# Sigmoid attention and two gated MLPs in one kernel: scores and value sums on one ring of four double PSUM banks, with fewer and longer bursts of sums

## The chip, the cores and the metric

The kernel runs on one core of a Trainium2 chip. The metric is the device time of one execution in microseconds (us), the median of several runs. The core's engines are named as in the profile: PE (TensorE, the matrix multiplies), DVE (VectorE), ACT (ScalarE), POOL (GpSimd) and SP (SyncE, which here only issues transfers). Each engine works through its own queue in order; one engine waits for another by counting semaphores. PSUM holds what PE writes; in this kernel it is handed out as "banks" of 512 floats per partition, eight in all, alone (`[P, 512]`) or as a double bank (`[P, 2, 512]`).

## The reference, cut to what matters

```
def attention(q, k, v):                        # q, k, v: (4 batches, 12 heads, 448, 64)
    scores = matmul(q, k.T) / sqrt(64) - log(448)
    return matmul(sigmoid(scores), v)          # no softmax, each weight stands alone

def gated_mlp(x, w_in, w_sp, b_sp, w_out, act):
    h = act(x @ w_in)                          # 768 -> 1024
    u, v = h[..., :512], h[..., 512:]
    v = (v - mean(v)) / sqrt(var(v) + 1e-6)    # the second MLP also: * g_ln
    v = einsum('ts,bsd->btd', w_sp, v) + b_sp[None, :, None]
    return (u * v) @ w_out                     # 512 -> 768

x = attention(q, k, v), heads side by side     # (4, 448, 768)
x = gated_mlp(x, ..., relu)
x = x + gated_mlp(x, ..., gelu_tanh)
```

## The kernel before, in words

**Parts.** Attention runs first. Then come the first MLP (`m1`) over the four batches, then a part in which the first MLP's output matrix and the second one's input matrix are multiplied into one, then the second MLP (`m2`). All products are of single-precision accuracy: most are made as three passes over operands split into a high part of a shorter format and a low part (`hi`, `lo`).

**Groups, pairs and units.** A *group* n is four heads of one batch (batch n // 3), so there are twelve; two groups n (even) and m = n + 1 make a *pair*, and there are six pairs. The 448 keys are cut into three row blocks of 128 and a rest of 64. A *unit* of scores (n, r) holds row block r of the four heads of a group, 24 matmuls (three passes by two halves of the head's 64 numbers by four heads, line 485). The rests of both groups of a pair are one unit of their own, (n, 3), 16 matmuls (line 503). So a pair has seven units, 42 in all. The very first unit, (0, 0), is made without splitting, from line 470.

**What follows a unit.** ACT takes the sigmoid of the unit's four banks with two instructions (`weigh`, line 452), which write the weights `a` (three buffers) or, for the rests, `ar` (one). PE then multiplies them with the values: `values(n, r, x)`, line 519, is a *slot* of two matmuls, for heads 2x and 2x + 1; x is the *half* of the group. Over r = 0, 3, 1, 2 a half's sums gather in one PSUM bank. When they are done, `gather(n, x)` lets ACT copy them (line 533) into a chunk of the next stage's input `x`. Even batches need one copy for a half; odd batches lie rotated in their tile and need four.

**Banks.** In attention two single banks (`ps_av`) hold the sums of the two halves, and three double banks (`ps_att`) hold scores, two for a unit. `ps_av` stays for the MLPs; `ps_att` is closed after the last unit of scores and its space is given to the pools `ps_sc` and `ps_t`.

**Order.** The order of PE's work in attention is written out by hand: a list `units` gives the order of the score units, and a table (`todo`, made into `sums`) says which slots of value sums stand behind each unit. The loop at the end of `attention` issues for each step s first `score(s)`, then `weigh_up(s)`, the *burst* of sums; then come DVE's preparation of later groups (`turn`: transposes; `high`, `low`: the split) and the next loads. PE runs its queue in the order in which it was issued.

**Weights.** The MLPs' weights arrive as 64-bit floats and are converted piece by piece by DVE and ACT. A `Belt` holds the jobs and each `tick` moves each running job on by a step and starts new ones. In attention the belt's jobs are `convert_early` (14 pieces of `w_in1`, at the steps that `rate` names); in the first MLP they are the pieces in `out1` (12 pieces of 256 columns of `w_out1`, stored to a matrix `flat` in DRAM), then those of `w_in2`, moved on by `fill`. `spatial` is such a belt for the matrix `w_sp`.

**The seam to the MLP.** After the last unit `done()` runs (`operands_made`): it closes attention's operand pool and `ps_att`, and issues the casts of the first batch's input (`split_x`: `xh` on ACT, `xl` on DVE). The last group's sums are copied by `gather_last`, which the program calls behind the first wide projection, `m1.hv(0, 0)` (18 matmuls, line 656):

```
            m1.hv(0, 0)
            gather_last()
            fill(1)
            for b in range(B):
                ...
                for j in range(0 if b else 1, J):
                    m1.hv(b, j)
                    fill(2 if j == J - 1 else 1)
```

`m1.hu` (line 702) makes the four blocks of `u` of a batch, `m1.sp` (line 722) the spatial product.

Of the kernel before, what the change touches and what calls it, by code (L numbers as in the profile page):

```python
# [9 lines left out]
F32 = mybir.dt.float32  # L10
# [16 lines left out]
def tile_sigmoid_attention_two_gated_mlps(  # L27
# [49 lines left out]
    ps_av = ctx.enter_context(tc.tile_pool(name="ps_av", bufs=2, space=bass.MemoryType.PSUM))  # L77
# [4 lines left out]
    xs = [const.tile([P, KF, 2 * S], F32, name=f"x{i}") for i in range(B // 2)]  # L82
    xe = [
        const.tile([P, KD - KF, 2 * S], F32, tag=f"xe{i}", name=f"xe{i}", bufs=1) for i in range(B // 2)
    ]

    def chunk_of(b, c):
        return xs[b // 2][:, c] if c < KF else xe[b // 2][:, c - KF]
# [9 lines left out]
    def av_bank():  # L98
        return ps_av.tile([P, 512], F32, tag="av", name="av")
# [54 lines left out]
    def convert_early(apool, src, n, size, part):  # L154
# [25 lines left out]
        f = f.bitcast(F32)  # L180
        hi, lo = part()
# [145 lines left out]
    out1 = pieces_kept(w_out1, 0, rows_of(flat))  # L327
# [4 lines left out]
    def attention(apool, epool, ps_att, done):  # L332
        G = H // 4
        NG = B * G
        raws, turned, ops, vs, att, avp = {}, {}, {}, {}, {}, {}

        def load_qk(n, xs="kq"):
            b, i = divmod(n, G)
# [9 lines left out]
        def load_v(n):  # L348
            b, i = divmod(n, G)
# [100 lines left out]
        def weigh(a, sc):  # L450
            for dst, src in sc:
                nc.scalar.activation(a[:, dst], src[..., :S], AF.Sigmoid, bias=bias_s, scale=scale)  # L452

        def pairs(sc):
            return [(slice(2 * x, 2 * x + 2), sc[x]) for x in range(2)]

        def scores(n, r):


            opk, opq = ops[n]  # L460
            if (n, r) == (0, 0):
                t, *av = ps_att.tile([P, 2, 512], F32, tag="sc", name="sc"), av_bank(), av_bank()
                banks = [t[:, 0], t[:, 1], *av]
                parts = [(2, av[0]), (3, av[1]), (slice(0, 2), t)]
# [11 lines left out]
            else:  # L476
                sc = score_banks()
                banks = [x[:, h] for x in sc for h in range(2)]
                parts = pairs(sc)
# [10 lines left out]
            att[n, r] = a = epool.tile([P, 4, S], F32, tag="a", name="a", bufs=3)  # L490
            weigh(a, parts)

        def scores_rest(n):


            sc = score_banks()
# [12 lines left out]
            weigh(a, pairs(sc))  # L509

        def values(n, r, x):
            if r == 0:
                avp[n, x] = av_bank()
            vt, vr = vs[n]
            at = REST * ((x + n) % 2)
            ps = slice(at, at + REST)
            for o in range(2):
                h = 2 * x + o
                nc.tensor.matmul(  # L519
                    avp[n, x][o * D:(o + 1) * D, :S],  # L520
                    vt[:, h, r] if r < 3 else vr[ps, o], att[n, r][:, h] if r < 3 else att[n, r][ps, h],
                    start=(r == 0), stop=(r == 2),
                )

        def gather(n, x):

            b, i = divmod(n, G)
            y = chunk_of(b, 2 * i + x)
            o = avp.pop((n, x))[:, :S].rearrange("p (c t) -> p t c", c=TC)

            def back(at, t0, t1, c0=0, c1=TC):
                dst = y[:, at:at + (t1 - t0) * (c1 - c0)]
                nc.scalar.copy(
                    out=dst.rearrange("p (t c) -> p t c", t=t1 - t0), in_=o[:, t0:t1, c0:c1]
                )
# [13 lines left out]
        for n in range(0, NG, 2):  # L549
            m, at = n + 1, len(units)  # L550
            units += [(n, 0), (n, 1), (n, 3), (n, 2), (m, 0), (m, 1), (m, 2)]
            both = lambda n, r: [(n, r, 0), (n, r, 1)]
            todo = (
                [(n, 0, 0)], [(n, 0, 1), (n, 1, 0)], [(n, 1, 1)] + both(n, 3), both(n, 2),
                both(m, 0), both(m, 3) + [(m, 1, 0)], [(m, 1, 1), (m, 2, 0)], [(m, 2, 1)],
            )
            if n == 0:
                todo = [both(0, r)[::-1] for r in (0, 1, 3, 2)] + list(todo[4:])
            for s, x in enumerate(todo, at + 1):
                sums.setdefault(s, []).extend(x)  # L560
# [27 lines left out]
        warm = av_bank()  # L588
# [31 lines left out]
        def gather_last():  # L620
            for x in range(2):
                gather(NG - 1, x)

        return gather_last


    class Mlp:
# [82 lines left out]
        def sp(self, b, i):  # L710
# [14 lines left out]
            if L.n == 1:  # L725
# [3 lines left out]
                    out=xs[b // 2][:, i, o:o + S], in0=t, in1=u, op=ALU.mult  # L729
# [397 lines left out]
```

## Time and profile before

| | |
|---|---|
| three runs | 556.13, 556.19, 556.82 us, median 556.19 |
| the profiled execution | 556.78 us, its span 555.0 us |
| busy share of the span | PE 99%, PEld (weight loads) 79%, DVE 65%, ACT 40%, POOL 6% |
| granted TensorE clock, mean | 0.999 |
| attention, 0 to 139.7 us | PE 138.35, DVE 107.16, ACT 96.51 us busy |
| first MLP, 139.7 to 291 us | PE 150.80, DVE 131.05, ACT 60.71 us busy |
| the two matrices made one, 291 to 324 us | PE 33.00, DVE 24.46, ACT 8.84 us busy |
| second MLP, 324 to 551.5 us | PE 227.49, DVE 96.96, ACT 54.90 us busy |

The times are those of one core, so the span is its span; 1.78 us of the profiled execution lie around it. A stage ends where PE's first matmul of the next one starts. Busy PE includes the time in which its pipeline fills and empties.

### The profile page before, as it was taken

How to read it: one execution, taken by the hardware profiler on the slowest of the kernel's cores; microseconds unless marked ns; L12 is line 12 of the kernel's file. 1: busy time of each engine (PE TensorE's matmuls, PEld its weight loads, DVE VectorE, ACT ScalarE, POOL GpSimd, SP SyncE). 2: the span in 40 equal slices, each digit the busy share in tenths (PEclk: the TensorE clock that was granted, in tenths of full speed). 3: DMA queues.
4: the chain of work that ended last, by engine and by line, in shares of the span. 5: the costliest groups of instructions: out<-in, count | busy, mean ns of one | idle time of the engine just before them, and what ended most of it. 6: DMA issues, size and time to landing. Idle time of an engine off the chain costs nothing.

```text
span 555.0 us, 9160 instructions
## 1 busy us (share of the span) xinstructions
PE 549.6 (99%) x3486; PEld 436.6 (79%) x3486; DVE 360.1 (65%) x753; ACT 221.0 (40%) x404; POOL 32.5 (6%) x62
## 2 busy tenths in 40 slices
PE   9999999999999999999999999999999999999997
PEld 5544445444798898898998889998999899989886
DVE  6999888850699999999865977951542264224311
ACT  5667676677434252361543156310320041113101
POOL 0000000000110100300100011000100020011000
PEclk9999999999999999999999999999999999999999
DMA  8788647200443265463445534200500032004003
GB/s 286 213 239 253 190 137 244 77 21 18 72 126 128 96 190 121 119 156 91 150 144 137 145 109 123 75 0 9 79 15 0 9 57 36 1 16 65 6 1 113
DMA packets 96107, 56.44 MB, mean 102 GB/s; under 512 B 67392, under 2 KB 84032, under 8 KB 96064
## 3 DMA queue, kind: packets, MB, share of 16 engines
q1 hardware_dynamic: 95920, 55.60, 37.0%
q8 instruction: 27, 0.44, 0.3%
q10 hardware_dynamic: 144, 0.26, 0.1%
q14 instruction: 16, 0.13, 0.1%
HBM read 44.83 MB, written 11.01 MB: 101 GB/s over the span
## 4 chain that ended last, share of the span: by engine, by line
PE 94%; DVE 2%; DMA 1%; issue 1%; ACT 1%; SPq 1%; POOL 0%; DVEq 0%; POOLq 0%; ACTq 0%
PE t L702 15%; PE t L656 14%; PE av L519 13%; PE sc L788 10%; PE sc L485 9%; PE t L722 6%; PE av L788 5%; PE av L722 3%; PE sc L722 3%; PE sc L798 3%; PE t L884 3%; PE av L884 3%; PE sc L503 2%; PE av L798 2%; PE t L798 2%; DMA w<-in_moe_w_out_dram 1%
## 5 line engine op out<-in xcount | busy, mean ns | idle before, releaser
L452 ACT ACTIVATE a<-sc,small 128x896 f32<-128x896 f32 x71 | 67.7, 1005 | 32.6 <-PE sc L485 32.6
L519 PE MATMUL av<-a,vt 128*64 128x448 f32 x288 | 63.0, 554 | 0.0
L485 PEld LDWEIGHTS sc<-opq,opk 32*128 32x128 f32 x840 | 38.4, 183 | 25.7 <-issue 13.4
L665 DVE BATCH_NORM_STATS2 st<-vr 128x6 f32<-128x512 f32 x28 | 19.4, 692 | 60.2 <-ACT vr L662 60.2
L485 PE MATMUL sc<-opq,opk 32*128 32x448 f32 x840 | 52.7, 378 | 0.0
L662 ACT ACTIVATE vr<-t 128x512 f32<-128x512 f32 x28 | 16.7, 596 | 84.3 <-PE t L656 80.5
L519 PEld LDWEIGHTS av<-a,vt 128*64 128x64 f32 x288 | 17.0, 136 | 32.2 <-issue 26.7
L656 PE MATMUL t<-vh,xh 128*128 128x512 f32 x112 | 41.4, 390 | 0.0
L732 DVE SCALAR_TENSOR_TENSOR gt<-t,bb 128x448 f32<-128x448 f32 x16 | 10.9, 681 | 45.3 <-PE t L722 45.3
L667 POOL TENSOR_SCALAR st<-st 128x1 f32<-128x1 f32 x28 | 10.8, 385 | 467.2 <-DVE st L666 467.2
L656 PE MATMUL t<-vh,xl 128*128 128x512 f32 x98 | 38.2, 389 | 0.0
L740 ACT CAST gh<-u 128x448 fp32r<-128x448 f32 (+1 forms) x16 | 8.6, 540 | 71.3 <-DVE u L736 71.3
L644 DVE TENSOR_TENSOR xl<-x,xh 128x512 fp32r<-128x512 f32 (+1 forms) x32 | 20.0, 653 | 24.0 <-ACT xh L643 23.8
L702 PE MATMUL t<-xh,uh 128*128 128x448 f32 x96 | 35.0, 364 | 0.5 <-ACT u L707 0.5
L702 PE MATMUL t<-xh,ul 128*128 128x448 f32 x96 | 34.8, 362 | 0.0
L702 PE MATMUL t<-xl,uh 128*128 128x448 f32 x96 | 34.6, 360 | 0.0
L722 PE MATMUL t<-sh,v 128*128 128x448 f32 x112 | 32.8, 362 | 0.0
L656 PE MATMUL t<-vl,xh 128*128 128x512 f32 x84 | 32.7, 389 | 0.0
L702 PE MATMUL t<-xh,vl 128*128 128x448 f32 x96 | 29.7, 363 | 0.0
L193 ACT ACTIVATE g<-w 128x256 f32<-128x256 f32 x48 | 20.1, 433 | 22.9 <-DMA w<-in_moe_w_out_dram 9.3
L684 ACT CAST v<-vr 128x512 fp32r<-128x512 f32 x24 | 14.9, 622 | 34.2 <-DVE vr L676 34.2
L656 PE MATMUL t<-m,xh 128*128 128x512 f32 x84 | 25.9, 390 | 0.0
(213 smaller groups left out, 1286.3 us busy)
## 6 DMA issues: line engine op xcount, KB each, us to landing
w<-in_moe_w_out_dram SPq DMA_DIRECT2D x24, 256.0 KB, 3.0
w<-in_moe_w_in_dram SPq DMA_DIRECT2D x24, 256.0 KB, 3.1
inq<-in_q_dram SPq DMA_DIRECT2D x12, 448.0 KB, 5.9
ink<-in_k_dram SPq DMA_DIRECT2D x11, 448.0 KB, 5.1
vt<-in_v_dram SPq DMA_DIRECT2D x48, 96.0 KB, 3.5
we<-in_moe_w_in_dram SPq DMA_DIRECT2D x6, 512.0 KB, 4.5
we<-in_moe_w_in_dram SPq DMA_DIRECT2D x8, 384.0 KB, 4.0
out_dram<-y SPq DMA_DIRECT2D x48, 56.0 KB, 1.9
```

Source lines behind the costliest of these rows:

```text
L193: nc.scalar.activation(g, high.bitcast(F32), AF.Square)
L452: nc.scalar.activation(a[:, dst], src[..., :S], AF.Sigmoid, bias=bias_s, scale=scale)
L485: nc.tensor.matmul(banks[h][:, :S], opk[ps, x, o:o + P], opq[ps, y, S * j:S * (j + 1)], start=(t == 0), stop=(t == 5), tile_position=(32 * ...
L519: nc.tensor.matmul(avp[n, x][o * D:(o + 1) * D, :S], vt[:, h, r] if r < 3 else vr[ps, o], att[n, r][:, h] if r < 3 else att[n, r][ps, h], ...
L644: nc.vector.tensor_tensor(out=pair[1][:, :n], in0=src, in1=raw(pair[0][:, :n]), op=ALU.subtract)
L656: nc.tensor.matmul(ps[:, :FF], a, w, start=(c == 0 and n == 0), stop=(c == self.kc - 1 and n == 2),)
L665: nc.vector.bn_stats(out=st, in_=vr)
L702: nc.tensor.matmul(ps[:, :S], w, a, start=(c == 0 and n == 0), stop=(c == self.kc - 1 and n == 2),)
L722: nc.tensor.matmul(ps[:, :S], a, w, start=(n == 0), stop=(n == len(todo) - 1))
L788: nc.tensor.matmul(self.o[m][:, :n_cols], w, a, start=(not second and i == 0 and n == 0), stop=(second and i == KF - 1 and n == 2),)
L798: nc.tensor.matmul(ps[:, :cols.stop - cols.start], a, w, start=(not second and i == 0 and n == 0), stop=(second and i == KF - 1 and n == 2),)
L884: nc.tensor.matmul(ps[:, :FF], x, w[:, c], start=(c == 0 and n == 0), stop=(c == KD - 1 and n == 2),)
```

## The change

**Banks.** `ps_av` goes out of attention. Four double banks, named by tags `s0` to `s3`, are handed out from a list, the `ring`: a unit of scores takes two and gives them back once weighed; a group's sums take one, with half 0 in its first bank and half 1 in its second, and give it back when both halves have been copied. Which bank stands where in the list is fixed when the program is written out. `a` gets a fourth buffer.

**Order.** In the pairs after the first, the rests' unit (n, 3) stands before (n, 1). Sums run in five bursts a pair, behind (n, 2), (m, 0) and (m, 2) and behind the first two units of the next pair. A slot of the rests now covers both halves. The copy of a half is issued with the slot that makes it full, inside the burst.

**Batches.** `place(n)` turns the order of batches to 1, 0, 3, 2. Odd batches are now copied by two instructions a half (392 and 70 columns) in place of four; the chunks' tiles are eight columns longer for it.

**Weights.** Four pieces of 384 columns of `w_out1` are converted in the last pair of attention (`convert_early` gets `dst`, and `rate` starts one at each of the steps 0 to 3 there) and stored to `flat`; the belt of the first MLP has six pieces of `w_out1` in place of twelve, and in batch 0 `fill` starts none between the wide projections.

**The seam.** `ps_att` is closed after all of attention, and `ps_t`, `ps_av` and `ps_sc` are opened there. The last group's copies belong to its bursts as all the others do, so they are issued before `m1.hv(0, 0)`, and behind `split_x`.

```diff
-    xs = [const.tile([P, KF, 2 * S], F32, name=f"x{i}") for i in range(B // 2)]
+    ROW, PAD = 2 * S, 8
+    xs = [const.tile([P, KF * ROW + PAD], F32, name=f"x{i}") for i in range(B // 2)]
...
+        if dst is not None:
+            nc.sync.dma_start(out=dst, in_=f)
+            return
...
+    soon = KF // 2
+    for c in range(soon):
+        rows = slice(c * P, (c + 1) * P)
+        for g in range(0, DM, 3 * P):
+            first.append((w_out1[rows, 2 * g:2 * (g + 3 * P)], 1, 3 * P, None, flat[rows, g:g + 3 * P]))
+    out1 = pieces_kept(w_out1, 0, rows_of(flat))[soon * (DM // PIECE):]
...
+        ring, open_sums = list(range(4)), {}
+
+        def banks_of(k, name):
+            return ps_att.tile([P, 2, 512], F32, tag=f"s{k}", name=name, bufs=1)
...
         def score_banks():
-            return [ps_att.tile([P, 2, 512], F32, tag="sc", name="sc") for _ in range(2)]
+            ks = [ring.pop(0) for _ in range(2)]
+            return ks, [banks_of(k, "sc") for k in ks]
+
+        def weigh(a, ks, sc):
+            for x in range(2):
+                dst = slice(2 * x, 2 * x + 2)
+                nc.scalar.activation(a[:, dst], sc[x][..., :S], AF.Sigmoid, bias=bias_s, scale=scale)
+            ring.extend(ks)
...
-            att[n, r] = a = epool.tile([P, 4, S], F32, tag="a", name="a", bufs=3)
-            weigh(a, parts)
+            att[n, r] = a = epool.tile([P, 4, S], F32, tag="a", name="a", bufs=4)
+            weigh(a, ks, sc)
...
         def values(n, r, x):
-            if r == 0:
-                avp[n, x] = av_bank()
+            if n not in open_sums:
+                k = ring.pop(0)
+                open_sums[n] = k, banks_of(k, "av"), [0, 0]
+            k, av, count = open_sums[n]
             vt, vr = vs[n]
...
+            xs = (x,) if r < 3 else (0, 1)
+            for x in xs:
+                at = REST * ((x + n) % 2)
+                ps = slice(at, at + REST)
+                for o in range(2):
+                    h = 2 * x + o
+                    nc.tensor.matmul(
+                        av[o * D:(o + 1) * D, x, :S],
+                        vt[:, h, r] if r < 3 else vr[ps, o], att[n, r][:, h] if r < 3 else att[n, r][ps, h],
+                        start=(count[x] == 0), stop=(count[x] == 3),
+                    )
+                count[x] += 1
+            for x in xs:
+                if count[x] == 4:
+                    gather(n, x, av[:, x])
+            if count == [4, 4]:
+                ring.append(k)
...
             if b % 2 == 0:
                 back(0, 0, 32)
             else:
-                t, c = divmod(3 * P, TC)
-                back(SPAN, 0, t)
-                back(SPAN + t * TC, t, t + 1, 0, c)
-                back(S, t, t + 1, c, TC)
-                back(S + TC - c, t + 1, 32)
+                t = 3 * P // TC
+                back(SPAN, 0, t + 1)
+                back(S - 3 * P % TC, t, 32)
...
-            units += [(n, 0), (n, 1), (n, 3), (n, 2), (m, 0), (m, 1), (m, 2)]
-            both = lambda n, r: [(n, r, 0), (n, r, 1)]
-            todo = (
-                [(n, 0, 0)], [(n, 0, 1), (n, 1, 0)], [(n, 1, 1)] + both(n, 3), both(n, 2),
...
+                units += [(n, 0), (n, 3), (n, 1), (n, 2)]
+                todo = {4: ((0, 0), (0, 1), (1, 0), (1, 1)), 5: ((3, 0), (2, 0), (2, 1))}
+            units += [(m, 0), (m, 1), (m, 2)]
+            then = {7: ((3, 0), (0, 0), (1, 0)), 8: ((1, 1), (2, 0)), 9: ((0, 1), (2, 1))}
...
-            return int(step in (0, 2, 5))
+            return int(step in ((0, 2, 5) if p < NG // 2 - 1 else range(4)))
...
-                if r == 2 and n < NG - 1:
-                    gather(n, x)
...
-        ps_att = tc.tile_pool(name="ps_att", bufs=3, space=psum)
+        ps_att = tc.tile_pool(name="ps_att", bufs=1, space=psum)
...
-            gather_last = attention(apool.__enter__(), epool, ps_att.__enter__(), operands_made)
+            last = attention(apool.__enter__(), epool, ps_att.__enter__(), operands_made)
+        ps_att.__exit__(None, None, None)
+        for x in ("ps_av", "ps_t", "ps_sc") if last == 0 else ("ps_t", "ps_av", "ps_sc"):
+            later[x] = ctx.enter_context(tc.tile_pool(name=x, bufs=2, space=psum))
...
             m1.hv(0, 0)
-            gather_last()
-            fill(1)
+            fill()
...
-                    fill(2 if j == J - 1 else 1)
+                    fill((2 if j == J - 1 else 1) if b else 0)
```

**What it does to the queues.** PE in the second pair, from its first unit of scores on. In these lists `sc` are scores, `av` sums, `a` and `ar` weights, `vt` and `vr` values; line 485 is now 500, 503 is 518, 519 is 538. Before:

```order
L485 MATMUL sc<-opq,opk 128x448 x24
L519 MATMUL av<-a,vt 64x448 x4
L485 MATMUL sc<-opq,opk 128x448 x24
L519 MATMUL av<-a,vt 64x448 x4
L503 MATMUL sc<-tq,tr 64x448 x16
L519 MATMUL av<-a,vt 64x448 x4
L485 MATMUL sc<-opq,opk 128x448 x24
L519 MATMUL av<-a,vt 64x448 x2
L519 MATMUL av<-ar,vr 64x448 x4
L485 MATMUL sc<-opq,opk 128x448 x24
L519 MATMUL av<-a,vt 64x448 x4
L485 MATMUL sc<-opq,opk 128x448 x24
```

And PE in the same pair after the change:

```order
L500 MATMUL sc<-opq,opk 128x448 x24
L538 MATMUL av<-a,vt 64x448 x4
L518 MATMUL sc<-tq,tr 64x448 x16
L538 MATMUL av<-a,vt 64x448 x4
L500 MATMUL sc<-opq,opk 128x448 x48
L538 MATMUL av<-a,vt 64x448 x8
L500 MATMUL sc<-opq,opk 128x448 x24
L538 MATMUL av<-ar,vr 64x448 x4
L538 MATMUL av<-a,vt 64x448 x4
L500 MATMUL sc<-opq,opk 128x448 x48
L538 MATMUL av<-ar,vr 64x448 x4
L538 MATMUL av<-a,vt 64x448 x4
```

Behind every unit of scores stood a burst; now two pairs of units stand together (48 matmuls), and one burst has eight matmuls.

PE in the burst behind (m, 0) of that pair, with the semaphores that each matmul waits for; the last four matmuls are row block 2 of half 0 and of half 1:

```order
L538 MATMUL av<-ar,vr 64x448 [waits DMAHW7_49,DMAHW0_49]
L538 MATMUL av<-ar,vr 64x448
L538 MATMUL av<-ar,vr 64x448 [waits DMAHW2_49,DMAHW1_49]
L538 MATMUL av<-ar,vr 64x448
L538 MATMUL av<-a,vt 64x448 x2
L538 MATMUL av<-a,vt 64x448 [waits Activation_49]
L538 MATMUL av<-a,vt 64x448
```

The first matmul of half 1 waits for a count of ACT. ACT beside it, the weighings of three units and the copies of the two halves (an odd batch, so two instructions a half):

```order
L473 ACTIVATE a<-sc,small 128x896 x6
L558 COPY xe_67<-av 128x392
L558 COPY xe_67<-av 128x70
L558 COPY xe_67<-av 128x392
L558 COPY xe_67<-av 128x70
```

The count is the one that ACT gives with the second COPY, the end of half 0's copy.

ACT at the end of attention, from the last two units' weighings. Before:

```order
L452 ACTIVATE a<-sc,small 128x896 x4
L643 CAST xh<-x_68 128x512 x4
L643 CAST xh<-xe_70 128x512 x2
L662 ACTIVATE vr<-t 128x512
L533 COPY xe_71<-av 128x378
L533 COPY xe_71<-av 128x6
```

And after the change:

```order
L473 ACTIVATE a<-sc,small 128x896 x4
L659 CAST xh<-x_65 128x512 x4
L659 CAST xh<-xe_67 128x512 x2
L558 COPY xe_68<-av 128x448 x2
L678 ACTIVATE vr<-t 128x512 x2
```

The last group's copies stand now before the first activation of the wide projection (`vr`), still behind the six casts. PE there, the last sums and the first two matmuls of the wide projection, before:

```order
L519 MATMUL av<-a,vt 64x448 [waits Activation_49]
L519 MATMUL av<-a,vt 64x448
L519 MATMUL av<-a,vt 64x448 [waits Activation_49]
L519 MATMUL av<-a,vt 64x448
L656 MATMUL t<-vh_76,xh 128x512 [waits PE_49,Activation_49]
L656 MATMUL t<-vl_77,xh 128x512
```

And after:

```order
L538 MATMUL av<-a,vt 64x448 [waits Activation_49]
L538 MATMUL av<-a,vt 64x448
L538 MATMUL av<-a,vt 64x448 [waits Activation_49]
L538 MATMUL av<-a,vt 64x448 x3
L672 MATMUL t<-vh_73,xh 128x512 [waits DMAHW3_49,DMAHW2_49,DMAHW4_49,DMAHW1_49,DMAHW5_49,DMAHW0_49,DMAHW6_49,DVE_49,Activation_49]
L672 MATMUL t<-vl_74,xh 128x512
```

Of the sums the last four matmuls are the slots (0, 1) and (2, 1) of half 1; the first of them waits for ACT's count of half 0's copy. The count that the projection's first matmul (line 672) waits for on ACT is that of half 1's copy.

## Rows read from the trace of the kernel before

**Rows 1.** The page, section 1: busy time, share of the span, instructions.
```profile
PE 549.6 (99%) x3486; PEld 436.6 (79%) x3486; DVE 360.1 (65%) x753; ACT 221.0 (40%) x404; POOL 32.5 (6%) x62
```

**Rows 2.** The chain in order of time, one pair: start us, us, engine, line, instructions.
```profile
48.88 1.42 PE sc L485 x21
50.31 1.66 PE av L519 x8
...
59.83 1.81 PE av L519 x12
...
71.05 1.42 PE sc L485 x21
```

**Rows 3.** Timeline of PE around two switches; start us, us, line, out<-in, instructions.
```profile
62.28 0.78 PE L485 MATMUL sc<-opq,opk 32*128 32x448 f32 x12
...
62.99 1.72 PE L519 MATMUL av<-a,vt 128*64 128x448 f32 x8
64.65 0.68 PE L485 MATMUL sc<-opq,opk 32*128 32x448 f32 x8
...
69.17 0.98 PE L519 MATMUL av<-ar,vr 64*64 64x448 f32 x8
...
70.08 0.97 PE L519 MATMUL av<-a,vt 128*64 128x448 f32 x4
```

**Rows 4.** Timeline of ACT beside it, weighings and copies; in brackets idle time before.
```profile
63.16 1.91 ACT L452 ACTIVATE a<-sc,small 128x896 f32<-128x896 f32 x2 [1.35 <-PE sc L485]
...
64.96 1.33 ACT L533 COPY x<-av 128x378 f32<-128x378 f32 x8
...
66.23 1.91 ACT L452 ACTIVATE a<-sc,small 128x896 f32<-128x896 f32 x2
```

**Rows 5.** Groups by form to 215 us: busy us, mean ns, idle before.
```profile
L533 ACT COPY x<-av 128x448 f32<-128x448 f32 x8 | 4.1, 539 | 0.0
...
L533 ACT COPY x<-av 128x378 f32<-128x378 f32 x8 | 3.9, 489 | 0.0
```

**Rows 6.** Timeline of the first pair: ACT, weight loads and PE.
```profile
9.33 2.81 ACT L452 ACTIVATE a<-sc,small 128x896 f32<-128x896 f32 x3
...
10.39 0.20 PEld L519 LDWEIGHTS av<-a,vt 128*64 128x64 f32 x4 [0.63 <-ACT a L452]
...
13.16 1.91 ACT L452 ACTIVATE ar<-sc,small 128x896 f32<-128x896 f32 x2 [1.02 <-PE sc L503]
...
16.98 1.75 PE L485 MATMUL sc<-opq,opk 32*128 32x448 f32 x24
```

**Rows 7.** Timeline of ACT, then PE, at the end of attention.
```profile
135.82 1.91 ACT L452 ACTIVATE a<-sc,small 128x896 f32<-128x896 f32 x2 [1.18 <-PE sc L485]
137.62 2.17 ACT L643 CAST xh<-x 128x512 fp32r<-128x512 f32 x4
...
136.58 3.23 PE L519 MATMUL av<-a,vt 128*64 128x448 f32 x16
139.74 0.50 PE L656 MATMUL t<-vh,xh 128*128 128x512 f32 x1
```

**Rows 8.** Timeline of PE in the fourth block of `u`.
```profile
166.79 0.37 PE L702 MATMUL t<-xh,ul 128*128 128x448 f32 x1
167.66 0.47 PE L702 MATMUL t<-xh,uh 128*128 128x448 f32 x1 [0.50 <-ACT u L707]
167.97 0.37 PE L702 MATMUL t<-xl,uh 128*128 128x448 f32 x1
```

**Rows 9.** Stretches: length, busy us (xcount) of PE, PEld, DVE, ACT, POOL, clock, DMA, GB/s.
```profile
14.00:28.00 14.00, 14.00 (x160) 7.24 (x156) 13.69 (x26) 9.56 (x12) 0.00 (x0) 1.00 0.78 216
...
112.00:126.00 14.00, 14.00 (x166) 6.82 (x164) 6.33 (x13) 9.31 (x17) 0.00 (x0) 1.00 0.03 7
...
553.00:554.00 1.00, 0.00 (x0) 0.00 (x0) 0.00 (x0) 0.00 (x0) 0.00 (x0) 0.77 0.42 146
```

More of the change, by code (lines that the diff above doesn't have):

```diff
@@ L98, in av_bank @@
     def av_bank():
-        return ps_av.tile([P, 512], F32, tag="av", name="av")
+        return later["ps_av"].tile([P, 512], F32, tag="av", name="av")
     class Layer:
@@ L152, in pieces_kept, with convert_early @@
         ]
[L154 removed]
+    def convert_early(apool, src, n, size, part, dst=None):
         w = apool.tile([P, FF, 2], I32, tag="we", name="we", bufs=3)[:, :size]
@@ L348, in load_v @@
         def load_v(n):
-            b, i = divmod(n, G)
+            b, i = place(n)
             vs[n] = vt, vr = (
@@ L447, in score_banks @@
         def score_banks():
-            return [ps_att.tile([P, 2, 512], F32, tag="sc", name="sc") for _ in range(2)]
[L450 to L455, printed above, removed]
+            ks = [ring.pop(0) for _ in range(2)]
[5 more added lines that the diff above has]
+            ring.extend(ks)
         def scores(n, r):
             opk, opq = ops[n]
+            ks, sc = score_banks()
+            banks = [x[:, h] for x in sc for h in range(2)]
             if (n, r) == (0, 0):
-                t, *av = ps_att.tile([P, 2, 512], F32, tag="sc", name="sc"), av_bank(), av_bank()
-                banks = [t[:, 0], t[:, 1], *av]
-                parts = [(2, av[0]), (3, av[1]), (slice(0, 2), t)]
                 tk, _, tq = turned[n]
@@ L508, in scores_rest, with gather, back @@
             att[n, 3] = att[n + 1, 3] = a = epool.tile([P, 4, S], F32, tag="ar", name="ar", bufs=1)
-            weigh(a, pairs(sc))
+            weigh(a, ks, sc)
         def values(n, r, x):
-            if r == 0:
-                avp[n, x] = av_bank()
+            if n not in open_sums:
+                k = ring.pop(0)
+                open_sums[n] = k, banks_of(k, "av"), [0, 0]
+            k, av, count = open_sums[n]
             vt, vr = vs[n]
[L515 to L527, printed above, removed]
-            y = chunk_of(b, 2 * i + x)
[L529 to L535, printed above, removed]
+            xs = (x,) if r < 3 else (0, 1)
[15 more added lines that the diff above has]
+                ring.append(k)
+        def gather(n, x, av):
+            b, i = place(n)
+            y = chunk_of(b, 2 * i + x)
+            o = av[:, :S].rearrange("p (c t) -> p t c", c=TC)
+            def back(at, t0, t1):
+                dst = y[:, at:at + (t1 - t0) * TC]
+                nc.scalar.copy(out=dst.rearrange("p (t c) -> p t c", c=TC), in_=o[:, t0:t1])
             if b % 2 == 0:
@@ L550, in attention @@
             m, at = n + 1, len(units)
-            units += [(n, 0), (n, 1), (n, 3), (n, 2), (m, 0), (m, 1), (m, 2)]
-            both = lambda n, r: [(n, r, 0), (n, r, 1)]
-            todo = (
-                [(n, 0, 0)], [(n, 0, 1), (n, 1, 0)], [(n, 1, 1)] + both(n, 3), both(n, 2),
-                both(m, 0), both(m, 3) + [(m, 1, 0)], [(m, 1, 1), (m, 2, 0)], [(m, 2, 1)],
-            )
-            if n == 0:
-                todo = [both(0, r)[::-1] for r in (0, 1, 3, 2)] + list(todo[4:])
-            for s, x in enumerate(todo, at + 1):
-                sums.setdefault(s, []).extend(x)
+            if n == 0:
+                units += [(n, 0), (n, 1), (n, 3), (n, 2)]
+                todo = {2: ((0, 0), (0, 1)), 3: ((1, 0),), 4: ((1, 1),), 5: ((3, 0), (2, 0), (2, 1))}
+            else:
+                units += [(n, 0), (n, 3), (n, 1), (n, 2)]
+                todo = {4: ((0, 0), (0, 1), (1, 0), (1, 1)), 5: ((3, 0), (2, 0), (2, 1))}
+            units += [(m, 0), (m, 1), (m, 2)]
+            then = {7: ((3, 0), (0, 0), (1, 0)), 8: ((1, 1), (2, 0)), 9: ((0, 1), (2, 1))}
+            for g, x in ((n, todo), (m, then)):
+                for s, items in x.items():
+                    sums.setdefault(at + s - 1, []).extend((g, *y) for y in items)
         U = len(units)
@@ L587, in attention @@
         later.pop("rows")()
-        warm = av_bank()
+        warm = banks_of(ring[-1], "av")[:, 0]
         for _ in range(9):
@@ L618, in attention @@
                 spatial.tick(1)
[L620 to L624, printed above, removed]
+        return open_sums[NG - 1][0]
     class Mlp:
@@ L728, in sp @@
                 nc.vector.tensor_tensor(
-                    out=xs[b // 2][:, i, o:o + S], in0=t, in1=u, op=ALU.mult
+                    out=chunk_of(b, i)[:, o:o + S], in0=t, in1=u, op=ALU.mult
                 )
```

25 lines of the change are left out of this document (11 added, 14 removed).

## The prediction

> **What bounds the kernel now.** I read the page first, then the chain of waits, then the timeline of TensorE (PE) and ScalarE (ACT) in the attention part, last the tables of busy time by stretch. PE is busy 99% of the span [rows 1], and the chain runs along PE from line to line with hardly a gap, so only PE's own work and PE's waits count. In attention the chain alternates between a unit of scores, 1.42 to 1.43 us, and a burst of value sums, 1.65 us, or 1.81 us where the burst holds sums of the remainder rows; a pair of groups takes 71.05 - 48.88 = 22.17 us [rows 2]. The busy share hides that the alternation has a price. Inside a unit three passes start at 62.28 and the last of them at 62.69, so a pass is 0.205 us; six are 1.23, and the unit's other 0.19 us is entry and exit. Four slots of value sums and the way back to scores are 64.65 - 62.99 = 1.66 us [rows 3]; sixteen instructions take 3.23 where eight take 1.72, so a slot is 0.377 [rows 3, 7], and 1.66 - 4 x 0.377 = 0.15 is again entry and exit. One alternation scores-sums-scores thus costs **0.34 us** beside its work.
>
> **The change, part by part.** The sum is made against the profiled execution, 556.78 us (span 555.0 and 1.78 around it), which lies 0.59 above the median of the three runs, 556.19; the difference is then put on the median.
>
> *Fewer alternations.* By the order, PE goes from scores to sums 41 times before (6 in the first pair, 7 in each of five) and 30 times after (5 in each of six pairs). 11 x 0.34 = -3.7 us. The work is the same. One burst more mixes remainder sums and whole ones, and a mix costs 1.81 - 1.65 = 0.16 [rows 2]: +0.2. No row shows two units of scores in a row; if the second one still paid its entry and exit, 10 or 11 x 0.19 = 2 us of the gain would be gone. I take the full gain, because inside a unit the next pass's weights come without a seam [rows 3].
>
> *Does ACT follow?* A weighing of one unit starts 66.23 - 64.65 = 1.58 us after its scores and frees ACT 64.96 - 63.16 = 1.80 us later [rows 3, 4]. A pair has seven, 12.6 us, and four copies of sums of some 0.55 to 0.67, together some 15 of the new 21.4 us. Walked through the ring of four in steady state, each double bank is free when PE wants it, with 0.2 us or more to spare but once (0.0 where the long burst takes the bank of the unit two before). In the first pair it is not: with shorter bursts there, PE reaches unit (0, 2) about 0.75 us earlier, finds the bank of the remainder scores still being weighed (before: from 13.16 [rows 6]), and the next unit finds the same. I get two waits of 0.3 to 0.4 against one of 0.25 before (16.98, 1.75 us where 1.50 is usual [rows 6]) and one short one at 10.39: **+0.3** (0 to 0.7).
>
> *The wait inside the burst.* Both halves of a group's sums now lie in one tile of two banks. The burst after (m, 0) runs: remainder sums, then row block 2 of half 0, the copy of half 0 on ACT, then row block 2 of half 1. In the built program the first matmul of half 1 waits for ACT, and the count it waits for is the one that the copy of half 0 gives (39 in the second pair; the second COPY of the odd batch has it). The program orders a read of the tile before the next write of it, though the halves are different banks. So PE stops in the middle of the burst until ACT has copied. Let T be the burst's start. Remainder sums take 0.91 (69.17 to 70.08 [rows 3]); the two slots of half 0 would let half 1 start at T + 0.91 + 0.80 = T + 1.71. The slots' end is T + 0.91 + 0.97 = T + 1.88; ACT, weighing (m, 0), is free at T + 1.97 (1.58 + 1.80 - 1.42 [rows 2 to 4]), so the copy starts there. It takes 0.54 for an even batch [rows 5]; for an odd one it is two pieces of 392 and 70 columns, an estimate of 0.67 (eight pieces of two chunks took 1.33 [rows 4], the large one 0.49 [rows 5]). PE follows an ACT end by 0.06 (first of three from 9.33, each 1.0; PE goes at 10.39 [rows 6]). Half 1 starts at T + 2.57 or T + 2.70: 0.87 or 0.99 us late. Two even and four odd pairs: 2 x 0.87 + 4 x 0.99 = **+5.7** (5.0 to 6.5). Who waits for it: all of PE's queue. In the odd groups of a pair the same wait stands between two bursts that have a unit of remainder scores between them; there the copy is done some 0.6 us earlier, so it costs nothing, except in the last group.
>
> *The end of attention.* In group 11 the copy of half 0 stands in ACT's queue behind the six casts of the next stage (`xh`), which the program issues when the operands' pool closes. Let S be the start of scores (11, 1); (11, 2) follows at S + 1.22. ACT weighs (11, 1) from S + 1.58, (11, 2) from S + 3.4, casts from S + 5.2, six at 2.17 / 4 apart [rows 7], and copies from about S + 8.3 to S + 8.88. PE has its other sums done at S + 6.62 and resumes at S + 8.94: **+2.3** (1.5 to 2.6). Then the first matmul of the next stage (`t`, the wide projection) waits for the copy of half 1, because all banks of the attention pool are closed at once; before, it followed the last sum at 139.74 directly [rows 7] and the copies came later. The last slot's end, 0.08, a copy of 0.54 and 0.06 against the usual seam: **+0.8** (0.6 to 0.9).
>
> *Converters.* Four pieces of 384 columns of `w_out1` move from the first MLP batch into the last pair, in place of six of 256. VectorE (DVE) has work for 6.33 of 14 us there [rows 9], so their some 2 us each are covered; their four loads and four stores on SP's queue come before the loads of `w_spatial`, which wait for the end of the scores anyway. Without the converters between the four wide projections, DVE reaches the last normalization sooner, ACT isn't held by it, and PE's one wait of that stage, 167.66 - 166.79 - 0.20 = 0.67 and 0.11 more at the next matmul [rows 8], goes: **-0.8** (0 to -0.8). What is late next there is nothing that I see; PE is dense before and after it. The kept pieces are still converted before batch 3 ends their use. Odd batches first, and two copies in place of four for them, change only loads and ACT's load, which has room: 0. The fourth `a` buffer is needed by the longer bursts, 0.
>
> Sum: -3.7 + 0.2 + 0.3 + 5.7 + 2.3 + 0.8 - 0.8 = **+4.8**; from 556.78 that is 561.6, on the median's footing 561.0.
>
> **Rivals.**
> *The halves go free* (faster). If the write of half 1 did not have to wait for the copy of half 0, in the bursts and at the end, the three plus terms 5.7, 2.3 and 0.8 vanish: -4.0, 552.2 us. It decides wherever ACT's copy ends before T + 1.71, or where the wait is not enforced. Against it: the wait is in the program, and ACT isn't even free before T + 1.97. Chance 0.07. The Trainium skill speaks for this rival, page "PSUM — Partial Sum Buffer", section "PSUM bank collisions raise a hardware error": "Semaphore-guard PSUM by bank × quadrant", since what collides is two engines in one bank. By that rule the chip needs no wait here and the sum would be -4.0; the program holds one all the same, and no row of before shows such a pair.
> *The clock falls at the end of attention.* PE is idle for some 2.3 us there. At the span's end, with no matmul running, the granted clock falls from 1.00 to 0.50 of 2.4 GHz within the stretch 553 to 554 [rows 9], soon after the last matmul. If it falls at S + 8, the 1.65 us of sums and some or all of the first wide projection (18 matmuls, 4.1 us) run at half speed: +1 to +4, I take +2: 563.0. For it: the fall at the end came without a long rest. Against: PE runs right up to the gap. Chance 0.2.
> *Scores behind scores keep their seam*: +2.0, 563.0. Chance 0.08.
> *Half the wait is hidden*, because ACT is freed earlier than the rows say or DVE's shorter list frees more: 557.5. Chance 0.05.
> *DVE becomes the bound in the early pairs*, where it is busy 13.69 of 14 us [rows 9]: its work per pair, some 21.8 us with the 512-column pieces, is no more than the new period with its wait, about 22.4, so this gives the forecast over again.
> That the change doesn't do what it says is excluded by the order: the bursts are merged there.
>
> **How the numbers follow.** The forecast has 0.60, around 561.0. The clock has 0.20 and the seam 0.08, both at 563; the half-hidden wait 0.05; free halves 0.07. The terms' own bounds give the forecast 559.4 to 562.2; to leave out no more than two in ten, the range takes in the 563 cases: 559.2 to 563.2. A measurement of this kernel can tell about 0.2% (1.1 us) from no change. Faster by more than that: free halves, 0.07. Within it: most of the half-hidden case and a tail of the forecast, 0.05. Slower: 0.88.
>
> **What the profile after would show.** Right: in the chain or among PE's waits, a wait of some 0.9 us on ACT's COPY (line 558) in every even group's burst, six in all, and one of over 2 us near the end of attention; two units of scores (48 matmuls) in about 2.65 us; a pair in some 22.3 us; the first wide projection starting near 145 instead of 139.74; no wait near the fourth `u` block. Wrong: no wait on line 558 and a pair of 21.4 us (free halves); a granted clock under 1.00 after the end of attention; 48 score matmuls in 2.85; a wait on DVE's transposes ahead of the remainder scores.

## The result and the profile after

The changed kernel takes **561.59 us** (median of four runs, 561.34 to 564.75) against 556.30 for the kernel before (four runs in the same comparison, 556.13 to 556.82): 1.0107 times as long, 95% interval 1.007 to 1.0143. Six more runs of it in a second set have a median of 561.85 against 556.48 (1.0118, interval 1.0093 to 1.0142). The profiled execution took 561.34 us, its span is 559.6, 4.6 more than that of before. In some runs of two kernels the granted clock falls for some microseconds; that is a finding of its own ("The clock in the gap"), and where it matters the text says which runs are compared.

Section 1 of the page after, beside [rows 1]. The columns are busy time, share of the span, instructions:

```profile
PE 547.8 (98%) x3486; PEld 438.6 (78%) x3486; DVE 359.6 (64%) x749; ACT 217.5 (39%) x373; POOL 32.5 (6%) x62
```

PE is busy 1.8 us less in a span 4.6 us longer: it waits where it did not. The waits of PE in the trace after (what was waited for, us in total, times, the longest one):

```profile
PE av L538 <- ACT xe L558: 3.5, 3, 2.0
PE av L538 <- ACT x L558: 2.8, 4, 0.7
PE av L610 <- POOL ident masks.py:199: 1.3, 1, 1.3
PE t L672 <- ACT xe L558: 0.6, 1, 0.6
PE av L538 <- ACT a L473: 0.2, 1, 0.2
```

Line 558 is the copy of sums. Seven waits for it come ahead of sums and one ahead of the wide projection (line 672); before, PE waited for no copy. The one wait of before in the first MLP [rows 8] is gone. The chain shows the new alternation, beside [rows 2] (start us, us, engine, line, instructions):

```profile
65.88 2.66 PE sc L500 x44
68.54 2.66 PE av L538 x16
...
88.40 2.68 PE sc L500 x46
...
110.92 2.68 PE sc L500 x45
```

A row that starts at 65.88 and the next of its kind at 88.40 and 110.92 are one place in three pairs: a pair takes 22.52 us, where before it took 22.17 [rows 2]. Two units of scores in a row (48 matmuls) take 2.66 to 2.68, twice six passes of 0.205 and one entry and exit.

The burst behind (m, 0) in the timeline, an even batch, beside [rows 3, 4]; in brackets the idle time before an instruction and what ended it:

```profile
62.37 0.98 PE L538 MATMUL av<-ar,vr 64*64 64x448 f32 x8
...
62.53 1.90 ACT L473 ACTIVATE a<-sc,small 128x896 f32<-128x896 f32 x2 [2.10 <-PE sc L500]
...
63.28 0.97 PE L538 MATMUL av<-a,vt 128*64 128x448 f32 x4
...
64.33 0.53 ACT L558 COPY x<-av 128x448 f32<-128x448 f32 x1
...
64.91 0.97 PE L538 MATMUL av<-a,vt 128*64 128x448 f32 x4 [0.66 <-ACT x L558]
...
65.81 2.52 PE L500 MATMUL sc<-opq,opk 32*128 32x448 f32 x44
```

Half 0's last matmuls start at 63.28, half 1's would start some 0.80 later; they start at 64.91, 0.83 late, 0.05 behind the copy of half 0 (64.33 and 0.53). The copy in turn starts when half 0 is done (63.28 and 0.97 make 64.25) and ACT, weighing (m, 0) from 62.53 on, is free.

The end of attention, beside [rows 7]:

```profile
136.97 3.23 PE L538 MATMUL av<-a,vt 128*64 128x448 f32 x16
...
138.47 2.19 ACT L659 CAST xh<-x 128x512 fp32r<-128x512 f32 x4
...
140.53 1.15 ACT L659 CAST xh<-xe 128x512 fp32r<-128x512 f32 x2
...
141.57 0.55 ACT L558 COPY xe<-av 128x448 f32<-128x448 f32 x1
...
142.17 1.72 PE L538 MATMUL av<-a,vt 128*64 128x448 f32 x8 [1.98 <-ACT xe L558]
...
143.94 0.53 ACT L558 COPY xe<-av 128x448 f32<-128x448 f32 x1 [1.83 <-PE av L538]
...
144.53 0.50 PE L672 MATMUL t<-vh,xh 128*128 128x512 f32 x1 [0.63 <-ACT xe L558]
```

The copy of half 0 (141.57) stands behind the six casts, the last eight instructions of sums start at 142.17 instead of some 140.0, and the wide projection at 144.53 waits for the copy of half 1. (The prediction's "slot" of 0.377 us is one pass of two instructions; a slot in the section on the kernel before is two of them.)

### The profile page after: what moved, and what is told of

It is laid out like the page before. It is cut to its first block, busy times and chain, and to the rows that moved or that the text cites. A ratio compares the mean times of both kernels' runs of the same rounds, so it can differ in the third digit from the quotient of the medians.

```text
span 559.6 us, 9090 instructions
## 1 busy us (share of the span) xinstructions
PE 547.8 (98%) x3486; PEld 438.6 (78%) x3486; DVE 359.6 (64%) x749; ACT 217.5 (39%) x373; POOL 32.5 (6%) x62
## 4 chain that ended last, share of the span: by engine, by line
PE 94%; ACT 4%; DMA 1%; DVE 0%; issue 0%; ACTq 0%
PE t L672 17%; PE t L718 17%; PE av L538 10%; PE sc L804 10%; PE sc L500 8%; PE t L738 6%; PE av L804 5%; PE av L738 3%; PE sc L738 3%; PE sc L814 3%; PE t L900 3%; PE av L900 3%; ACT a L473 3%; PE sc L518 2%; PE av L814 1%; PE t L814 1%
## 5 line engine op out<-in xcount | busy, mean ns | idle before, releaser
L500 PEld LDWEIGHTS sc<-opq,opk 32*128 32x128 f32 x840 | 39.8, 183 | 17.9 <-issue 12.7
L500 PE MATMUL sc<-opq,opk 32*128 32x448 f32 x840 | 49.9, 373 | 0.0
L723 ACT ACTIVATE u<-t 128x448 f32<-128x448 f32 x32 | 17.4, 544 | 24.9 <-PE t L718 24.7
```

What stands on the lines that cost most here:

```text
L500: nc.tensor.matmul(banks[h][:, :S], opk[ps, x, o:o + P], opq[ps, y, S * j:S * (j + 1)], start=(t == 0), stop=(t == 5), tile_position=(32 * ...
L723: nc.scalar.activation(u, ps[:, :S], AF.Relu if L.n == 1 else AF.Gelu_apprx_tanh)
```

## Experiments

All times are compared with runs of the kernel before on the same chip, whose median was 556.31, 556.48 and 556.31 in the three sets. To compare places in traces, the stretch from the first burst of sums (9.56 us before, 8.65 after, 9.25 in end_only, 9.45 in free_end) to the first wide projection (139.74, 144.53, 142.22 and 136.90) is used: 130.18 us before, 135.88 after.

**Copies behind the burst (late_copy).** `values` only notes a finished half; the copies are issued after the burst's last matmul.

```diff
...
-                    gather(n, x, av[:, x])
+                    full.append((n, x, av[:, x]))
...
                 values(n, r, x)
+            while full:
+                gather(*full.pop(0))
```

> The changed kernel, but in each burst the copies of sums are issued after the burst's last matmul, so half 1 no longer stands behind the copy of half 0 (except in the last group, whose two halves lie in different bursts). Theory (the order of copy and write in one tile is the cost): the five waits of 0.88 to 0.96 us inside the bursts behind (m, 0), and that of the first pair, go; six waits, 2 x 0.88 + 4 x 0.96 = 5.6 us, so 561.6 - 5.6 = 556.0, and a pair takes some 21.6 instead of 22.5. The wait of about 2 us at the end of attention stays. Rival (ACT and the ring of banks can't follow the longer bursts): the waits come back at the banks of the next units, and the time stays above 559.

Ten runs, five of them at a mean clock of 1.000 with a median of 556.65 (555.89 to 556.74) and five at 0.994 to 0.997 (558.21 to 559.11). At full clock that is 0.3 above before, where the changed kernel's full-clock runs are 5.1 and 5.3 above in its two sets: 4.8 to 4.9 us came back, where 5.6 was expected. PE's waits for copies, all that are left:

```profile
PE av L538 <- ACT xe L558: 2.0, 1, 2.0
...
PE t L674 <- ACT xe L558: 0.6, 1, 0.6
```

The six waits inside the bursts are gone, and only the two at the end of attention are left on line 558. The order of copy and write in one tile was the cost, and ACT and the ring follow.

**The last group alone (end_only).** The bursts are as in the changed kernel; the last group's copies stand behind the first wide projection, and each double bank has a pool of its own, so that three of them can be closed before the last one.

```diff
...
-                if count[x] == 4:
+                if count[x] == 4 and n < NG - 1:
                     gather(n, x, av[:, x])
+                elif count[x] == 4:
+                    full.append((n, x, av[:, x]))
...
-        ps_att = tc.tile_pool(name="ps_att", bufs=1, space=psum)
+        ps_att = {k: tc.tile_pool(name=f"ps_r{k}", bufs=1, space=psum, side="right" if k == 1 else "left") for k in range(4)}
...
             m1.hv(0, 0)
+            gather_last()
+            ps_att[last].__exit__(None, None, None)
...
```

> The changed kernel with its copies inside the bursts as they are, but the last group's copies behind the first wide projection, and the four double banks in pools of their own so that this projection doesn't wait for them. Theory: only the wait of 2.2 us ahead of the last sums and the 0.8 us ahead of the projection go: 561.6 - 3.0 = 558.6. Rival (the six casts hold the projection anyway, since it needs their results): the projection starts no earlier than the second cast of the inputs ends, and 1 us or less comes back, 560.6 or more.

559.12 us, 2.8 above before: 2.3 to 2.5 came back, where 3.0 was expected. Its trace takes 132.97 us from the first burst to the wide projection, 2.9 less than the changed kernel's 135.88 (but its first burst starts 0.6 later, at 9.25, behind a wait that the trace after does not have), and the last sums run in one piece:

```profile
137.56 4.73 PE L538 MATMUL av<-a,vt 128*64 128x448 f32 x24
...
139.06 2.19 ACT L667 CAST xh<-x 128x512 fp32r<-128x512 f32 x4
...
141.13 1.16 ACT L667 CAST xh<-xe 128x512 fp32r<-128x512 f32 x2
...
142.22 0.50 PE L680 MATMUL t<-vh,xh 128*128 128x512 f32 x1
```

The projection starts behind the sums while the casts are just done: they did not hold it. This run takes both waits at the end away at once, so what each is worth by itself is read from the trace after, not from a run.

**Both edits (free_end).**

> Both edits together: copies after the burst, the last group's behind the first wide projection. Theory: the savings add up, 561.6 - 5.6 - 3.0 = 553.0, some 3.3 below the kernel before, and no wait of PE on ACT's copies is left in the trace. Rival (the merged bursts gain nothing, the old alternation was hidden): 556.3 less the 0.8 of the first MLP, 555.5 or more. If the dips of the granted clock that one of the changed kernel's four runs shows come from the gap at the end of attention, no run of this kernel shows one.

553.63 us, 0.995 times the kernel before (interval 0.9938 to 0.9963), 0.6 above what was expected. No wait for a copy is left:

```profile
PE av L612 <- POOL ident masks.py:199: 1.3, 1, 1.3
PE av L538 <- ACT a L473: 0.2, 1, 0.2
```

From the first burst to the projection it takes 127.45 us, 2.7 less than before and 8.4 less than the changed kernel. So the merged bursts do gain, and the change had hidden it. A pair from the chain:

```profile
69.22 1.43 PE sc L500 x23
...
75.65 2.68 PE sc L500 x45
...
85.49 2.71 PE sc L500 x40
...
90.81 1.43 PE sc L500 x22
```

It takes 90.81 - 69.22 = 21.59 us, 0.58 less than before, where two alternations at 0.34 promise 0.68. Of the difference 0.09 is in the two rows of double units, 2.68 and 2.71 where twelve passes and one entry and exit come to 2.65.

**The converters alone (conv_before).** The kernel before with the changed kernel's `dst`, `soon`, `rate` and `fill` lines, and nothing else.

> The kernel before with one part of the change alone: the four pieces of w_out1 converted in the last pair, six pieces left for the first MLP, none started in batch 0 between the wide projections. Theory: the wait of 0.67 us in the fourth u block goes with its 0.11, 556.3 - 0.8 = 555.5, and attention stays at 139.74 us. Rival (the saving in the first MLP came with the new place of the last copies, not with the converters): 556.3.

555.25 us, 0.998 times before (interval 0.9971 to 0.9989), 1.06 less. PE's wait for line 707 is gone from the list of waits:

```profile
PE av L598 <- POOL ident masks.py:199: 1.3, 1, 1.3
```

**The old order on the ring (seven_bursts).** free_end with the order of before:

```diff
...
+            units += [(n, 0), (n, 1), (n, 3), (n, 2), (m, 0), (m, 1), (m, 2)]
+            both = lambda n, r: [(n, r, 0), (n, r, 1)] if r < 3 else [(n, r, 0)]
+            todo = (
+                [(n, 0, 0)], [(n, 0, 1), (n, 1, 0)], [(n, 1, 1)] + both(n, 3), both(n, 2),
+                both(m, 0), both(m, 3) + [(m, 1, 0)], [(m, 1, 1), (m, 2, 0)], [(m, 2, 1)],
+            )
...
```

> The kernel free_end (553.6) with the order of the kernel before on the ring of four: units (n, 0), (n, 1), (n, 3), (n, 2), (m, 0) to (m, 2) and a burst of sums behind each, 41 alternations where free_end has 30. Theory (each alternation costs 0.34 us beside its work): 553.6 + 11 x 0.34 - 0.2 = 557.1, and a pair takes 22.2 us. Rival (the gain of the merged bursts came from something else, the ring or the fourth weight buffer): 554 or less.

558.88 us, 2.4 above before; against free_end, each taken beside its own runs of before, 5.1 more, where 3.5 was expected. The trace shows what the sum had left out: the unit of the rests is longer.

```profile
74.68 1.43 PE sc L500 x22
76.11 1.65 PE av L538 x8
77.77 2.14 PE sc L518 x32
79.91 1.65 PE av L538 x8
```

```profile
78.16 0.60 PEld L518 LDWEIGHTS sc<-tq,tr 32*64 32x64 f32 x22 [0.27 <-ACT a L473]
```

The unit takes 2.14 us, where it takes 1.69 in these pairs of before, of the changed kernel and of free_end: inside it the weight loads wait for ACT. By the program both double banks that this unit takes are those of the unit just before, (n, 1), and it waits for both of its weighings; with the three banks of before it shared one with it. So this run is a test of the alternation only after 0.45 a pair is taken off: 94.22 - 71.60 = 22.62 us, less 0.45 is 22.17, the pair of before. That leaves 0.58 for the two alternations, as the steady pair of free_end had it; the subtraction is worked out and was not run. That the old order on the new ring is slower than on the old banks was not expected. That the gain came from the ring or the fourth buffer, which this run also has, is excluded.

**The place of the tiles (before_pad8).** After 291 us nothing was to differ, yet from the second MLP's first matmul to the end the changed kernel's profiled execution takes 231.9 us where before it took 231.3. Its wide projections are longer, with no wait. The kernel before with only the tiles of `x` eight columns longer:

```diff
-    xs = [const.tile([P, KF, 2 * S], F32, name=f"x{i}") for i in range(B // 2)]
+    ROW, PAD = 2 * S, 8
+    xs = [const.tile([P, KF * ROW + PAD], F32, name=f"x{i}") for i in range(B // 2)]
...
```

> The kernel before with nothing changed but the tiles of x, eight columns longer as in the changed kernel, which moves the tiles behind them. In the changed kernel's trace the four wide projections of the second MLP take 0.17 to 0.25 us longer each (11.15, 8.36, 11.15, 8.37 where before has 10.92, 8.18, 10.90, 8.20), 0.83 together, with no wait. If the place of the operands in the on-chip memory does it, this kernel shows the same in its trace and takes 556.3 + 0.8 = 557.1. If it is the place of the sums (other PSUM banks) or something else of the change, the projections stay at 10.9 and 8.2 and the time at 556.3.

557.27 us, 1.0013 times before (interval 1.0005 to 1.0022), 0.8 more. The first of the projections (48 matmuls) in the chain of the changed kernel and of this one:

```profile
327.66 11.15 PE t L672 x48
```

```profile
323.25 11.15 PE t L658 x48
```

It is the place of the tiles, not the banks of the sums: this kernel's PSUM is that of before. Which of the tiles that move it is, was not tried.

**The order of the batches (batches_in_order), and the pad away (in_order_pad0).** free_end with `place(n)` returning batch and group in order and the four copies of an odd half as before; then the same with `PAD = 0`.

> The kernel free_end with the batches in the order 0, 1, 2, 3 and the odd ones copied by four instructions a half again. Theory (the order of batches and the number of copies change only loads and ACT's load, which has room): 553.6, within 0.3, and no new wait of PE. Rival (the longer copies hold a bank or a weighing): PE waits for ACT in the odd pairs, and up to 1.5 us are lost, 555.1.

> The kernel batches_in_order (553.9) without the eight columns behind the tiles of x, which its copies don't need. Theory (the place of the tiles costs the wide projections 0.8 us): they take 10.9 and 8.2 us again in the second MLP, and the time is 553.9 - 0.8 = 553.1, some 3.3 below the kernel before. Rival (the other PSUM banks of this kernel cost the same by themselves): 11.15 and 8.36, and 553.9.

553.94 us (0.9953, interval 0.994 to 0.9966) against free_end's 553.63 (0.995): the batches' order and the number of copies change nothing that shows. Without the eight columns **553.13 us**, 0.9943 times before (interval 0.9931 to 0.9956), the fastest kernel here. By the runs alone the step from batches_in_order lies within the two intervals; the row for the projection shows it:

```profile
320.11 10.92 PE t L682 x48
```

## The clock in the gap

**The changed kernel again (after_again).**

> The changed kernel as it is, for the granted clock. One of its four runs took 564.75 at a mean clock of 0.994 and the kernel late_copy did so in five of ten; its trace has the fall right in the gap of PE ahead of the first wide projection, while the kernels without that gap show none in nine runs. Theory (the gap lets the clock fall, in some runs): some runs near 561.5 at 1.0 and some 2.5 to 3.2 above at 0.994. Rival (chance of that chip or job): no more than one run below 0.998.

Four runs from 561.46 to 561.87 at 0.999 or 1.0, and two, 565.54 and 565.01, at 0.994. With the four of the first comparison that makes three of ten, 3 to 4 us above the others. The profiled executions of the changed kernel are none of them, but that of late_copy is one of its five. Its granted clock by stretch (length, busy us of PE, PEld, DVE, ACT, POOL, then the clock, DMA share, GB/s):

```profile
136.00:138.00 2.00, 1.29 (x8) 0.48 (x8) 1.36 (x3) 0.66 (x2) 0.00 (x0) 0.98 0.57 85
138.00:140.00 2.00, 1.37 (x5) 0.50 (x2) 0.00 (x0) 0.53 (x1) 0.00 (x0) 0.50 0.03 8
...
144.00:146.00 2.00, 2.00 (x9) 1.58 (x8) 0.00 (x0) 0.00 (x0) 0.00 (x0) 0.81 0.00 0
146.00:148.00 2.00, 2.00 (x11) 1.62 (x10) 0.95 (x3) 0.60 (x1) 0.00 (x0) 1.00 0.00 0
```

PE had just waited 2.0 us for the copy of half 0; the clock falls to 0.50 (1.2 GHz) within the last sums, just before 138, stays there in the two stretches left out, and is back at 1.00 (2.4 GHz) some 6.8 us later, with PE at the projection from 139.42 on. PE had been at the sums again for some 1.2 us when the clock fell, and the second wait, for the copy at 138.84, had not begun, so in this trace the second wait did not lead to the fall:

```profile
136.71 2.09 PE L538 MATMUL av<-a,vt 128*64 128x448 f32 x8 [1.99 <-ACT xe L558]
...
138.84 0.53 ACT L558 COPY xe<-av 128x448 f32<-128x448 f32 x1 [2.18 <-PE av L538]
```

A matmul of the projection takes 0.63 us in that stretch and 0.39 behind it:

```profile
140.01 0.63 PE L674 MATMUL t<-vl,xh 128*128 128x512 f32 x1
...
145.22 0.39 PE L674 MATMUL t<-vh,xl 128*128 128x512 f32 x1
```

The Trainium skill, page "TensorE: Matmul & The Clock Gate", section "HAM oscillation — how this bites in real kernels", tells of matmul stretches that start at the half rate because a wait ahead of them let the clock fall. The trace agrees in that the projection starts at the half rate behind waits (0.63 us against 0.39); the sums between the two waits started at the full one, and the clock fell while they ran. That the clock falls in some runs only of the same program is what the runs here add.

**One gap (one_gap).** late_copy with both copies of the last group behind its last sum.

> The kernel late_copy, but both copies of the last group are issued after its last sum. The wait of 2.0 us ahead of the last sums goes; the first wide projection still waits for the copies of the two halves, which follow one another: the later sums end some 0.1 us before ACT is free of the casts, two copies of 0.55 and 0.06 on top, a wait of some 1.2 us. Theory: 553.6 (free_end) + 1.2 = 554.8, and runs at a mean clock of 0.994 are rare or gone, because it takes the two gaps together (2.0 and, two slots of sums later, 0.6 us in late_copy's trace) to let the clock fall. Rival (any gap of about a microsecond there lets it fall): again three or more of ten runs lie 2.4 us above the others, at 0.994.

554.49 us (554.11 to 555.0, ten runs, all at 0.999 or 1.0), 0.9969 times before (interval 0.996 to 0.9979). PE waits once, ahead of the projection:

```profile
PE t L676 <- ACT xe L558: 1.1, 1, 1.1
```

1.1 us of waiting did not let the clock fall in ten runs, nor did free_end and end_only, without the gap, in nine; 2.0 us and a second gap of 0.6 did in eight of twenty. One_gap shortens the long wait as well as doing away with the second one, so the runs don't say that it takes both, as was expected, and the trace above speaks for the long one. One_gap also ran on a chip on which neither kernel with the 2.0 us ran, so a difference between chips isn't excluded for its ten; free_end and end_only ran on the chip of late_copy.

## Why the prediction was right, point by point

The forecast was 561.0 (559.2 to 563.2); measured was 561.59. Most terms hold one by one:

- *Wait inside the burst, +5.7.* In the trace the first matmul of half 1 starts 0.82 us late in the two even batches and 0.87 to 0.90 in the four odd ones (start to start of single instructions, less 0.377), 5.2 together, where 0.87 and 0.99 were put down; the two copies of an odd half take 0.60, not 0.67. Taking the waits away gave 4.8 to 4.9 back: the mechanism is shown by late_copy.
- *End of attention, +2.3 and +0.8.* By the starts of single instructions 2.1 and 0.7; end_only gives 2.9 back in its trace.
- *Both together* were 8.8; after against free_end it is 135.88 - 127.45 = 8.4.
- *Alternations, mixes and first pair, -3.7 + 0.2 + 0.3 = -3.2.* Measured is 127.45 - 130.18 = -2.7. This step was mis-sized: the steady pair gains 0.58, not 0.68. The 0.5 is made up by the 0.4 that the waits fell short, which is luck.
- *Converters, -0.8.* First MLP: 290.83 - 139.74 = 151.09 us before, 294.80 - 144.53 = 150.27 after, -0.82. conv_before shows the cause alone.
- *Batches, number of copies: 0.* Shown by batches_in_order. The fourth `a` buffer, also put at 0, was not tried by itself.

Two things of about 0.8 us were missing, and they cancel in the profiled execution. The eight columns of pad cost 0.8 (before_pad8); the prediction has no term for the longer tiles and put the copies that they serve at 0. And the very first unit of scores took 1.69 us (5.53 to 7.22) where it took 2.66 in the trace of before; over the twelve traces here it takes 1.69 to 2.66 in kernels of either kind (free_end 2.53, before_pad8 1.86), so nothing ties this to the change. It may be why the median of the runs is above the forecast (561.59 against 561.0) and the profiled execution is not (561.34 against 561.6): the prediction took 0.59 off for the median because the profiled execution of before, with its long first unit, lay that far above it. No run settles that.

Of the rivals, *the halves go free* is excluded by the waits on line 558. *Scores behind scores keep their seam* is excluded by 2.66 us for 48 matmuls. *The clock falls at the end of attention*, given 0.2 and +2, is what three of ten runs of the changed kernel do, at +3 to +4; its size was put too low, and those runs (564.75 to 565.54) lie above the range. *Half the wait is hidden* did not happen. The rule of the Trainium skill that was weighed there, page "PSUM — Partial Sum Buffer", section "PSUM bank collisions raise a hardware error", guards by bank and quadrant: what the program enforced was by tile, and PE waited. No run here let PE write one bank of a tile while ACT read the other: in free_end ACT's copy starts only when the burst's last matmul is done, as the row at 85.53 shows with PE's burst from 83.76:

```profile
83.76 1.72 PE L538 MATMUL av<-a,vt 128*64 128x448 f32 x8
...
85.53 1.12 ACT L558 COPY x<-av 128x392 f32<-128x392 f32 x4 [0.62 <-PE av L538]
```

## What to carry to other kernels

Two halves that are written and read at different times belong in different tiles, or the reads belong behind the last write; only the second was tried. Here the order of four lines was worth nearly 5 us, more than the whole gain that the change was after. When pools are closed together, the next stage waits for the last reader of any of them; look at which instruction gives the count that the first matmul waits for, and what is queued ahead of it on its engine. A change of a tile's length moves every tile behind it, so compare stages that the change should not touch as well.

## What was not expected of the hardware

The same 48 matmuls of the wide projection take 10.92 or 11.15 us by the place of the tiles alone (0.2275 or 0.2323 us each), with no wait in the trace. The clock's fall in a gap of PE of 2.0 us comes in some runs of a program and not in others, lasts some 6.8 us and costs 2.2 us in late_copy (median of five runs against median of five) and 3 to 4 in the changed kernel. And in the first unit of scores of the kernel before matmuls take 1.01 us at its start and 0.54 at its end, and the row of the stretch has a granted clock of 1.00 all the while:

```profile
5.49 1.01 PE L470 MATMUL sc<-tq,tk 32*64 32x448 f32 x2
...
7.67 0.54 PE L470 MATMUL sc<-tq,tk 32*64 32x448 f32 x2
```

```profile
6.00:7.00 1.00, 1.00 (x16) 0.38 (x8) 1.00 (x3) 0.60 (x2) 0.00 (x0) 1.00 0.95 228
```

In the five traces in which the unit takes 1.69 us its matmuls have the short times from the start; in the seven others they pass from the long to the short ones within it, at a place that differs from trace to trace.

The Trainium skill's page "TensorE: Matmul & The Clock Gate", section "Seeing it yourself", warns that recorded events of the clock can be unreliable; these rows fit that, but no run here was made to tell it from another cause.
